# One of VectorE's three operations moved to GpSimd for some score tiles, and the last softmax denominators spread by a shuffle, in an attention block on one core

## The chip, the cores and the metric

The kernel runs on one core of a Trainium2 chip. The metric is the time of one execution on the device in microseconds (us). A profile's span is about 1.8 us shorter than that time. A run over 1.5% above the fastest of its kernel would be called slow. The granted clock of TensorE is the share of its full clock that the trace says it was given.

## The reference

A multi-head attention block, S = 2048 tokens, D = 448, 16 heads of 28:

```python
qkv = (x @ wqkv).reshape(B, S, 3, H, Dh)        # -> q, k, v per head
scores = einsum("bhqd,bhkd->bhqk", q, k) * (Dh ** -0.5)
p = softmax(scores, axis=-1)
o = einsum("bhqk,bhkd->bhqd", p, v)
return o.reshape(B, S, D) @ wo                  # inputs and output bf16
```

## The kernel before

The work is cut into 16 windows (4 groups of 4 heads, times 4 blocks of 512 queries). A window has 16 x 4 = 64 score tiles of 128 keys by 512 queries, 1024 tiles in all. Each tile needs an exponential. ScalarE does most of them, two tiles per instruction (an "exp" below). The others, the "VectorE tiles", go through a cubic polynomial that makes the bits of a bf16 number directly. A VectorE tile takes three VectorE operations and one GpSimd product:

```python
p1 = DVE  tensor_scalar:         DU = SIG/65536 * lo + SIG*(SS - 0.5)      # lo: low 16 bits of the score in PSUM
p2 = DVE  scalar_tensor_tensor:  DV = (lo + const) * DU
gq = POOL tensor_tensor:         DG = DV * DU
f  = DVE  scalar_tensor_tensor:  PTD = (score + const) + DG                # frees the PSUM bank
```

Three PSUM banks (PD) hold VectorE tiles, two double banks (PA) hold pairs for ScalarE, and one bank (PO) collects P times V of a window; its row 28 of each head's 32 rows holds the softmax denominator. The order of all instructions on each engine is fixed while the program is built, by a list scheduler inside the kernel that assumes durations.

The ending of the last window is written by hand. It gathers partial denominators early, so that after the last exp only a reciprocal of 128x16 numbers is left, spread by fp32 matmuls:

```python
for j in range(NKT - NLAST, NKT):            # the last 3 key blocks
    ...                                      # 16 one-column matmuls add to the denominators, then 4 PV matmuls
nc.vector.reciprocal(out=RT[:], in_=gb[:, 0:TPC * HG])       # 128x16
den_expand(0, nc.vector.tensor_copy); den_expand(1, nc.scalar.copy)
...                                          # fp32 matmuls with an identity spread them over the rows
for hf in range(2):
    nc.vector.tensor_tensor(out=OTL[hf][:], in0=OH[hf][:], in1=spread[hf], op=ALU.mult)
    ...                                      # output matmuls; then 2 additions (VectorE), 2 copies (ScalarE), 4 DMAs
```

The softmax here doesn't subtract the row's maximum and nothing guards it: scores larger than these inputs give would overflow.

Of the kernel before, what the change touches and what calls it, by code (L numbers as in the profile page):

```python
# [75 lines left out]
def kernel(  # L76
# [29 lines left out]
    J0 = 10  # L106
    NTAIL = 12
    JL = 6
    DI = 2
    WPE = 1  # L110
    PVM = 0.0
    ADUR = 0.25
# [7 lines left out]
    QEA = 30  # L120
# [6 lines left out]
    O1 = 30  # L127
    O2 = 10
    OF = 0.4
    RV = 2  # L130
# [4 lines left out]
    SPLIT = {2: 4, 3: 2}  # L135
# [3 lines left out]
    UO = 40  # L139

# [32 lines left out]
    DG = [sb([P, QW], F16, f"DG{i}") for i in range(NB)]  # L173
    PARTL = [sb([P, D], F32, f"PARTL{i}") for i in range(2)]
# [15 lines left out]
    ident32 = sb([P, P], F32, "ident32")  # L190
    sel = sb([P, HG], F32, "sel")
    OH = [sb([P, QW // 2], F32, f"OH{i}") for i in range(2)]
    RT = sb([P, TPC * HG], F32, "RT")
    RX = [sb([P, QW // 2], F32, f"RX{i}") for i in range(2)]
# [31 lines left out]
    nc.gpsimd.memset(sel[:], 0.0)  # L226
    for i in range(HG):
        nc.gpsimd.affine_select(out=sel[:, i:i + 1], in_=sel[:, i:i + 1], compare_op=ALU.not_equal,
                                fill=1.0, base=-(HP * i + Dh), pattern=[[0, 1]], channel_multiplier=1)
    nc.gpsimd.memset(ident32[:], 0.0)  # L230
    nc.gpsimd.affine_select(out=ident32[:], in_=ident32[:], compare_op=ALU.not_equal,
                            fill=1.0, base=0, pattern=[[-1, P]], channel_multiplier=1)
# [345 lines left out]
    gbank = [None]  # L578

    def hold(t):  # L580
        free = [s for s in d_slots if s.free_at <= t + 1e-9]
        if free:
            free[0].free_at = 1e18
            gbank[0] = free[0].idx
        return bool(free)

# [7 lines left out]
    def task_part(c, n):  # L594
        due = (12 + c) * WT - PARTD
        for tq in range(n):
# [35 lines left out]
    NLAST = 3  # L632
    NROW = NW * NKT - NLAST
# [24 lines left out]
    def chain_A(fn, deps, acq=None):  # L658
        prev = None
        for tq in range(TPC):  # L660
            prev = add(Op("PE", ADUR, lambda tq=tq: fn(tq), deps=[prev] if prev else deps, prio=-5000 + tq, kind="A",
                          lat=PLAT if tq == TPC - 1 else 0.0, acq=acq if tq == 0 else None))
        return prev

    def den_gather(dst, src, tqs=range(TPC)):
        for tq in tqs:
            nc.tensor.matmul(out=dst[:, tq * HG:(tq + 1) * HG], lhsT=src(tq), rhs=sel[:], start=(tq == 0), stop=True,
                             skip_group_check=True)

    def den_expand(hf, copy):  # L670
        n = TPC * HG // 2
        copy(out=RX[hf][:].rearrange("p (n e) -> p n e", e=HP),
             in_=RT[:, hf * n:(hf + 1) * n].rearrange("p (n o) -> p n o", o=1).to_broadcast([P, n, HP]))

    def den_spread(dst, tqs=range(TPC)):
        for tq in tqs:
            nc.tensor.matmul(out=dst[:, tq * P:(tq + 1) * P], lhsT=RX[tq // 2][:, (tq % 2) * P:(tq % 2 + 1) * P],
                             rhs=ident32[:], start=True, stop=True)

    def partial_sums(pvop):  # L680
        ev = add(Op("DVE", 0.62, lambda: nc.vector.tensor_copy(out=OSB[(NW - 1) % 2][:], in_=PO[:]), deps=[pvop], prio=-5000))
        chain_A(lambda tq: den_gather(PD[gbank[0]], lambda k: OSB[(NW - 1) % 2][:, k * P:(k + 1) * P], (tq,)), [ev], hold)

    def finish_window(w, t):
# [11 lines left out]

        if w >= NW - WPE:
            ev.after = None
            d1 = chain_A(lambda tq: den_gather(PO, lambda k: OSB[b][:, k * P:(k + 1) * P], (tq,)), [ev])
            d2 = add(Op("DVE", 0.17, lambda: nc.vector.reciprocal(out=RT[:], in_=PO[:, 0:TPC * HG]), deps=[d1], prio=-5000))  # L700
            d2a = [add(Op("DVE", 0.25, lambda hf=hf: den_expand(hf, nc.vector.tensor_copy), deps=[d2], prio=-5000)) for hf in range(2)]
            d2b = chain_A(lambda tq: den_spread(PO, (tq,)), d2a)
            d3 = add(Op("DVE", 0.62, lambda: nc.vector.tensor_tensor(out=OT[g][c][:], in0=OSB[b][:], in1=PO[:], op=ALU.mult),
                        deps=[d2b], prio=-5000))
            d3.after = rel
            norm_busy[b] = d3
            ot_done[(g, c)] = d3
            if g == G - 2 and c in SPLIT:
                task_part(c, SPLIT[c])
            if g == G - 1:  # L710
                task_OP(c)
            return
# [19 lines left out]
    def start_tile(n, sop, slot, t):  # L732
# [5 lines left out]
        lo = PX[slot.idx][:].bitcast(U16).rearrange("p (n two) -> p n two", two=2)[:, :, 0]  # L738
        p1 = add(Op("DVE", P1, lambda: nc.vector.tensor_scalar(  # L739
            out=DU[b][:], in0=lo, scalar1=SIG / 65536, scalar2=SIG * (SS - 0.5), op0=ALU.mult, op1=ALU.add),  # L740
            deps=[sop] + prevl, prio=n - O1))
        p2 = add(Op("DVE", P1, lambda: nc.vector.scalar_tensor_tensor(  # L742
            out=DV[b][:], in0=lo, scalar=65536 * (SS - 0.5 + CE / C3), in1=DU[b][:], op0=ALU.add, op1=ALU.mult),
            deps=[p1], prio=n - O2, lat=0.22))
# [377 lines left out]
```

## Time and profile before

| | before |
|---|---|
| time, first 4 runs | 415.99 us median (415.77 to 416.25) |
| span of the profiled run | 414.2 us |
| busy ScalarE / VectorE / TensorE / GpSimd | 97% / 95% / 89% / 54% |
| exps on ScalarE, VectorE tiles | 424, 176 |
| last exp ends, ending after it | 405.21 us, 9.0 us |

The first lines of the page give busy time, share of the span and instructions per engine (PEld is TensorE's weight loading).

```profile
PE 366.8 (89%) x2679; PEld 124.9 (30%) x2679; DVE 395.1 (95%) x699; ACT 399.9 (97%) x439; POOL 224.9 (54%) x210
...
ACT 82%; PE 9%; issue 6%; DMA 1%; DVE 1%; SPq 0%; DVEq 0%
```

The second line is the chain that ended last, by engine: 82% of the span is ScalarE. The table of stretches says why (columns: stretch, its length, then busy time and number of instructions per engine, granted clock of TensorE, share of DMA time, GB/s).

```profile
core 0: us, PE busy (x) PEld busy (x) DVE busy (x) ACT busy (x) POOL busy (x), PEclk, DMA share, GB/s
20.00:400.00 380.00, 338.64 (x2428) 108.87 (x2424) 373.50 (x644) 380.00 (x416) 218.91 (x191) 1.00 0.13 30
...
409.00:411.00 2.00, 0.98 (x6) 0.29 (x3) 1.27 (x3) 0.97 (x2) 0.00 (x0) 1.00 0.02 7
```

ScalarE is busy 380.00 of 380.00 us. VectorE, at 373.50, is nearly full as well. That looks like two bounds, but only one can be read as such: an exp starts every 0.916 us without a gap, so nothing that VectorE or GpSimd does late makes ScalarE wait here. The granted clock reads 1.00. In the view of waits, GpSimd waits for VectorE:

```profile
POOL DG_181 L745 <- DVE DV_175 L742: 35.6, 22, 9.4
```

(35.6 us in total, 22 times, longest 9.4; five more buffers have 23.6 to 29.1 us each.) Last, the ending in order of time (start, duration, engine, line, operation, output<-inputs, number, and in brackets the idle time before it with what ended it).

```profile
403.92 1.29 ACT L934 ACTIVATE PTA_131<-PA_200 128x1024 bf16<-128x1024 f32 x1
...
406.70 0.39 PE L1073 MATMUL PO<-PTA_131,VA_110 128*32 128x512 bf16 x2
406.80 0.26 DVE L1075 RECIPROCAL RT<-PD_201 128x16 f32<-128x16 f32 x1 [1.04 <-PE PD_201 L1069]
...
409.44 0.54 PE L1062 MATMUL PA_199<-WO,OTL_220 128*128 128x448 bf16 x2
...
411.01 0.38 ACTq L1094 DMA_DIRECT2D out_dram<-OUTF_218  x1
```

The last exp ends at 403.92 + 1.29 = 405.21 us; the last PV matmul at 407.09; the span at 414.2.

### The profile page before, as it was taken

The numbers are of one execution on the slowest core, as the hardware profiler recorded it, in microseconds if no ns is written. First come the engines' busy times: TensorE is split into PE (matmuls) and PEld (weight loads), VectorE is DVE, ScalarE is ACT, GpSimd is POOL, SyncE is SP. The second block draws the span as 40 slices with busy tenths as digits, with TensorE's granted clock in tenths as the row PEclk, the third lists the DMA queues.
The fourth block names the chain that finished last, engine by engine and source line by source line (L and its number), as shares of the span: only waits on it lengthen the run. The fifth ranks groups of instructions, "written<-read, shape, count | busy, mean of one in ns | idle before, by whom it ended". The sixth has DMA issues, their size and how long they took to land.

```text
span 414.2 us, 7679 instructions
## 1 busy us (share of the span) xinstructions
PE 366.8 (89%) x2679; PEld 124.9 (30%) x2679; DVE 395.1 (95%) x699; ACT 399.9 (97%) x439; POOL 224.9 (54%) x210
## 2 busy tenths in 40 slices
PE   8988989898898889898897988889898988889995
PEld 5433222323232233323222222222322222222233
DVE  6899999999999999999999999999999999999974
ACT  4999999999999999999999999999999999999992
POOL 3155556474656547475555646456475656656440
PEclk9999999999999999999999999999999999999999
DMA  8410020202201011111400001010410101001012
GB/s 258 80 16 21 3 50 8 55 21 60 65 2 46 0 33 25 26 32 25 97 6 29 18 18 31 2 40 6 91 34 2 46 2 36 10 27 47 18 55 90
DMA packets 33414, 15.85 MB, mean 38 GB/s; under 512 B 26016, under 2 KB 30304, under 8 KB 33376
## 3 DMA queue, kind: packets, MB, share of 16 engines
q1 hardware_dynamic: 32304, 15.05, 14.5%
q8 instruction: 21, 0.34, 0.4%
q10 hardware_dynamic: 1072, 0.32, 0.3%
q14 instruction: 17, 0.14, 0.1%
HBM read 7.37 MB, written 1.96 MB: 23 GB/s over the span
## 4 chain that ended last, share of the span: by engine, by line
ACT 82%; PE 9%; issue 6%; DMA 1%; DVE 1%; SPq 0%; DVEq 0%
ACT PTA_131 L934 4%; ACT PTA_132 L934 4%; ACT PTA_133 L934 4%; ACT PTA_134 L934 4%; ACT PTA_145 L934 4%; ACT PTA_136 L934 4%; ACT PTA_135 L934 4%; ACT PTA_140 L934 4%; ACT PTA_144 L934 3%; ACT PTA_137 L934 3%; ACT PTA_141 L934 3%; ACT PTA_149 L934 3%; ACT PTA_148 L934 3%; ACT PTA_139 L934 3%; ACT PTA_138 L934 3%
## 5 line engine op out<-in xcount | busy, mean ns | idle before, releaser
L745 POOL TENSOR_TENSOR DG_181<-DV_175,DU_169 128x512 f16<-128x512 f16 x30 | 34.6, 1154 | 35.8 <-DVE DV_175 L742 35.6
L745 POOL TENSOR_TENSOR DG_182<-DV_176,DU_170 128x512 f16<-128x512 f16 x30 | 34.6, 1153 | 29.7 <-DVE DV_176 L742 29.1
L745 POOL TENSOR_TENSOR DG_184<-DV_178,DU_172 128x512 f16<-128x512 f16 x29 | 33.5, 1154 | 29.8 <-DVE DV_178 L742 28.5
L745 POOL TENSOR_TENSOR DG_185<-DV_179,DU_173 128x512 f16<-128x512 f16 x29 | 33.4, 1153 | 25.9 <-DVE DV_179 L742 25.8
L745 POOL TENSOR_TENSOR DG_186<-DV_180,DU_174 128x512 f16<-128x512 f16 x29 | 33.5, 1154 | 24.9 <-DVE DV_180 L742 24.7
L745 POOL TENSOR_TENSOR DG_183<-DV_177,DU_171 128x512 f16<-128x512 f16 x29 | 33.4, 1153 | 23.7 <-DVE DV_177 L742 23.6
L649 PEld LDWEIGHTS <-KB_1_94 64*128 64x128 bf16 x256 | 20.8, 93 | 48.2 <-issue 47.3
L649 PEld LDWEIGHTS <-KB_0_91 64*128 64x128 bf16 x256 | 20.5, 93 | 45.8 <-issue 42.1
L649 PEld LDWEIGHTS <-KB_1_92 64*128 64x128 bf16 x256 | 20.2, 93 | 45.8 <-issue 43.9
L649 PEld LDWEIGHTS <-KB_0_93 64*128 64x128 bf16 x256 | 20.5, 93 | 43.8 <-issue 42.7
L934 ACT ACTIVATE PTA_145<-PA_199 128x1024 bf16<-128x1024 f32 x18 | 22.6, 1254 | 0.0
L934 ACT ACTIVATE PTA_144<-PA_200 128x1024 bf16<-128x1024 f32 x18 | 22.5, 1250 | 0.0
L934 ACT ACTIVATE PTA_140<-PA_200 128x1024 bf16<-128x1024 f32 x18 | 22.5, 1249 | 0.0
L934 ACT ACTIVATE PTA_143<-PA_199 128x1024 bf16<-128x1024 f32 x18 | 22.4, 1247 | 0.0
L934 ACT ACTIVATE PTA_139<-PA_199 128x1024 bf16<-128x1024 f32 x18 | 22.4, 1246 | 0.0
L934 ACT ACTIVATE PTA_142<-PA_200 128x1024 bf16<-128x1024 f32 x18 | 22.4, 1242 | 0.0
L934 ACT ACTIVATE PTA_138<-PA_200 128x1024 bf16<-128x1024 f32 x18 | 22.3, 1241 | 0.0
L934 ACT ACTIVATE PTA_141<-PA_199 128x1024 bf16<-128x1024 f32 x18 | 22.3, 1240 | 0.0
L739 DVE TENSOR_SCALAR DU_171<-PD_203 128x512 f16<-128x512 uint16 x29 | 19.9, 685 | 1.0 <-PE PD_203 L649 0.7
L739 DVE TENSOR_SCALAR DU_172<-PD_201 128x512 f16<-128x512 uint16 x29 | 19.8, 682 | 0.9 <-PE PD_201 L649 0.9
L739 DVE TENSOR_SCALAR DU_169<-PD_201 128x512 f16<-128x512 uint16 x29 | 19.8, 684 | 0.5 <-PE PD_201 L649 0.5
L742 DVE SCALAR_TENSOR_TENSOR DV_178<-PD_201,DU_172 128x512 f16<-128x512 uint16 x29 | 19.9, 686 | 0.3
(618 smaller groups left out, 1515.5 us busy)
## 6 DMA issues: line engine op xcount, KB each, us to landing
RRB_195<-SCR_197 SPq DMA_DIRECT2D x8, 256.0 KB
RRB_196<-SCR_198 SPq DMA_DIRECT2D x7, 256.0 KB
KB_1_94<-KB_0_93 SPq DMA_DIRECT2D x4, 128.0 KB
XS_127<-in_x_dram SPq DMA_DIRECT2D x1, 448.0 KB
XS_128<-in_x_dram SPq DMA_DIRECT2D x1, 448.0 KB
XS_129<-in_x_dram SPq DMA_DIRECT2D x1, 448.0 KB
XS_130<-in_x_dram SPq DMA_DIRECT2D x1, 448.0 KB
out_dram<-XS_127 SPq DMA_DIRECT2D x1, 448.0 KB
```

The costliest lines, as they stand in the source:

```text
L649: nc.tensor.matmul(out=ap, lhsT=KB[g % 2][i // 2][a:a + 64, j * P:(j + 1) * P], rhs=QB[w % NQB][i // 2][a:a + 64, :], start=True, stop=Tru ...
L739: p1 = add(Op("DVE", P1, lambda: nc.vector.tensor_scalar(out=DU[b][:], in0=lo, scalar1=SIG / 65536, scalar2=SIG * (SS - 0.5), op0=ALU.mult ...
L742: p2 = add(Op("DVE", P1, lambda: nc.vector.scalar_tensor_tensor(out=DV[b][:], in0=lo, scalar=65536 * (SS - 0.5 + CE / C3), in1=DU[b][:], o ...
L745: gq = add(Op("POOL", PTT, lambda: nc.gpsimd.tensor_tensor(out=DG[b][:], in0=DV[b][:], in1=DU[b][:], op=ALU.mult), deps=[p2], prio=n, kind ...
L934: nc.scalar.activation(out=PTA[pslot.idx][:, 0:len(ns) * QW], in_=PA[s.idx][:, 0:len(ns) * QW], func=ACT.Exp, bias=ACT_BIAS, scale=ACT_SCALE)
```

## The change

The intent: VectorE is nearly as full as ScalarE while GpSimd idles, so for some VectorE tiles GpSimd makes the whole cubic factor and VectorE drops its second operation. A tile is chosen for this when little GpSimd work is queued (XTH), and none of the last 60 tiles is (XEND). In the ending the gathering of denominators and the fp32 matmuls go; VectorE spreads the denominator row by a shuffle inside each group of 32 rows and takes the reciprocal of 128x256 numbers, twice. Four numbers of the scheduler change with it (J0, QEA, O1, RV), and the first three groups' share of the last output rows is partly summed in PSUM (late_sums).

```diff
-    J0 = 10
+    J0 = 9
-    QEA = 30
+    QEA = 20
-    O1 = 30
+    O1 = 20
-    RV = 2
+    RV = 4
+    XTH = 1.5
+    XEND = 60
 ...
+        if pool_load(t) < XTH and n < NT - XEND:
+            p1 = DVE  tensor_scalar   DU = lo/65536 + (SS - 0.5)
+            ga = POOL tensor_scalar   DW = C3*DU + CE
+            gs = POOL tensor_tensor   DV = DU * DU
+            gq = POOL tensor_tensor   DV = DV * DW
+        else:
             p1, p2, gq as before (the product now in place, in DV)
 ...
-    for j in range(NKT - NLAST, NKT): ...          # early denominators, reciprocal of 128x16, fp32 matmuls
     for hf in range(2):
+        cols = slice(hf * hw, (hf + 1) * hw)
+        nc.vector.stream_shuffle(out=DEN[hf][:], in_=PO[:, cols], mask=[Dh] * HP)
+        nc.vector.reciprocal(out=DEN[hf][:], in_=DEN[hf][:])
+        nc.vector.tensor_tensor(out=OTL[hf][:], in0=PO[:, cols], in1=DEN[hf][:], op=ALU.mult)
         for tq in (2 * hf, 2 * hf + 1):
+            nc.tensor.matmul(out=fb[tq], lhsT=OTL[hf][...], rhs=WO[:, g, :], start=(tq not in late_acc), stop=True)
```

(The four operations of the new tile are abbreviated; the rest is cut.)

More of the change, by code (lines that the diff above doesn't have):

```diff
@@ L105 @@
     PBACK = 3
-    J0 = 10
+    J0 = 9
     NTAIL = 12
     JL = 6
+    JACC = 8
     DI = 2
-    WPE = 1
     PVM = 0.0
-    ADUR = 0.25
     PLD = 0.2
@@ L134 @@
     MG = 0.1
-    SPLIT = {2: 4, 3: 2}
+    SPLIT = {2: (0, 1, 2, 3), 3: (2,)}
+    ACCQ = (0, 1, 3)
+    ACCP = 2000
     PARTD = 60
@@ L139 @@
     UO = 40
+    XTH = 1.5
+    XEND = 60
+    PTA1 = 0.62
+    PTQ = 1.04
     x2 = x[0]
@@ L172 @@
     DV = [sb([P, QW], F16, f"DV{i}") for i in range(NB)]
-    DG = [sb([P, QW], F16, f"DG{i}") for i in range(NB)]
-    PARTL = [sb([P, D], F32, f"PARTL{i}") for i in range(2)]
+    DG = DV
+    DW = [sb([P, QW], F16, f"DW{i}") for i in range(2)]
+    PARTL = {tq: sb([P, D], F32, f"PARTL{tq}") for tq in SPLIT[NQC - 1]}
     OSB = [sb([P, QW], F32, f"OSB{i}") for i in range(2)]
@@ L189 @@
     zrow = sb([P, QW], BF16, "zrow")
-    ident32 = sb([P, P], F32, "ident32")
-    sel = sb([P, HG], F32, "sel")
-    OH = [sb([P, QW // 2], F32, f"OH{i}") for i in range(2)]
-    RT = sb([P, TPC * HG], F32, "RT")
-    RX = [sb([P, QW // 2], F32, f"RX{i}") for i in range(2)]
+    DEN = [sb([P, QW // 2], F32, f"DEN{i}") for i in range(2)]
     OUTF = [sb([P, D], BF16, f"OUTF{i}") for i in range(TPC)]
@@ L225 @@
                                 base=-(HP * i + Dh), pattern=[[0, 1]], channel_multiplier=1)
-    nc.gpsimd.memset(sel[:], 0.0)
-    for i in range(HG):
-        nc.gpsimd.affine_select(out=sel[:, i:i + 1], in_=sel[:, i:i + 1], compare_op=ALU.not_equal,
-                                fill=1.0, base=-(HP * i + Dh), pattern=[[0, 1]], channel_multiplier=1)
-    nc.gpsimd.memset(ident32[:], 0.0)
-    nc.gpsimd.affine_select(out=ident32[:], in_=ident32[:], compare_op=ALU.not_equal,
-                            fill=1.0, base=0, pattern=[[-1, P]], channel_multiplier=1)
     for g in range(G):
@@ L576 @@
     ot_done = {}
-    gbank = [None]
-    def hold(t):
-        free = [s for s in d_slots if s.free_at <= t + 1e-9]
-        if free:
-            free[0].free_at = 1e18
-            gbank[0] = free[0].idx
-        return bool(free)
     parts = {}
@@ L595, in task_part @@
         due = (12 + c) * WT - PARTD
-        for tq in range(n):
+        for tq in n:
             task = bank_task()
@@ L631 @@
     NW = G * NQC
-    NLAST = 3
-    NROW = NW * NKT - NLAST
+    NROW = NW * NKT
     rows = {}
@@ L655, in s_ready @@
                 and kmrep[(g, j // TPC, i)].done(t))
-    def chain_A(fn, deps, acq=None):
-        prev = None
-        for tq in range(TPC):
-            prev = add(Op("PE", ADUR, lambda tq=tq: fn(tq), deps=[prev] if prev else deps, prio=-5000 + tq, kind="A",
-                          lat=PLAT if tq == TPC - 1 else 0.0, acq=acq if tq == 0 else None))
-        return prev
-    def den_gather(dst, src, tqs=range(TPC)):
-        for tq in tqs:
-            nc.tensor.matmul(out=dst[:, tq * HG:(tq + 1) * HG], lhsT=src(tq), rhs=sel[:], start=(tq == 0), stop=True,
-                             skip_group_check=True)
@@ L670, in den_expand @@
-    def den_expand(hf, copy):
-        n = TPC * HG // 2
-        copy(out=RX[hf][:].rearrange("p (n e) -> p n e", e=HP),
-             in_=RT[:, hf * n:(hf + 1) * n].rearrange("p (n o) -> p n o", o=1).to_broadcast([P, n, HP]))
-    def den_spread(dst, tqs=range(TPC)):
-        for tq in tqs:
-            nc.tensor.matmul(out=dst[:, tq * P:(tq + 1) * P], lhsT=RX[tq // 2][:, (tq % 2) * P:(tq % 2 + 1) * P],
-                             rhs=ident32[:], start=True, stop=True)
-    def partial_sums(pvop):
-        ev = add(Op("DVE", 0.62, lambda: nc.vector.tensor_copy(out=OSB[(NW - 1) % 2][:], in_=PO[:]), deps=[pvop], prio=-5000))
-        chain_A(lambda tq: den_gather(PD[gbank[0]], lambda k: OSB[(NW - 1) % 2][:, k * P:(k + 1) * P], (tq,)), [ev], hold)
+    late_acc = {}
@@ new lines, in late_sums, with take, f @@
+    def late_sums():
+        def take(tq, n):
+            def f(t):
+                if pos[0] < NT - NTAIL or n and any(o.kind == "B" and o.acq is not None for o in static["PE"]):
+                    return False
+                free = [x for x in d_slots if x.free_at <= t + 1e-9]
+                if not free:
+                    return False
+                free[0].free_at = 1e18
+                late_acc[tq] = free[0].idx
+                return True
+            return f
+        prev = None
+        for n, tq in enumerate(ACCQ):
+            for gg in range(G - 1):
+                prev = add(Op("PE", 0.19, lambda tq=tq, gg=gg: nc.tensor.matmul(
+                    out=PD[late_acc[tq]][:, 0:D], lhsT=OT[gg][NQC - 1][:, tq * P:(tq + 1) * P], rhs=WO[:, gg, :],
+                    start=(gg == 0), stop=False), deps=([prev] if prev else []) + [ot_done[(g_, NQC - 1)] for g_ in range(G - 1)],
+                    prio=ACCP + tq + 0.1 * gg, kind="A", lat=0.0, acq=take(tq, n) if gg == 0 else None))
@@ L695, in finish_window @@
         ev.after = rel
-        if w >= NW - WPE:
-            ev.after = None
-            d1 = chain_A(lambda tq: den_gather(PO, lambda k: OSB[b][:, k * P:(k + 1) * P], (tq,)), [ev])
-            d2 = add(Op("DVE", 0.17, lambda: nc.vector.reciprocal(out=RT[:], in_=PO[:, 0:TPC * HG]), deps=[d1], prio=-5000))
-            d2a = [add(Op("DVE", 0.25, lambda hf=hf: den_expand(hf, nc.vector.tensor_copy), deps=[d2], prio=-5000)) for hf in range(2)]
-            d2b = chain_A(lambda tq: den_spread(PO, (tq,)), d2a)
-            d3 = add(Op("DVE", 0.62, lambda: nc.vector.tensor_tensor(out=OT[g][c][:], in0=OSB[b][:], in1=PO[:], op=ALU.mult),
-                        deps=[d2b], prio=-5000))
-            d3.after = rel
-            norm_busy[b] = d3
-            ot_done[(g, c)] = d3
-            if g == G - 2 and c in SPLIT:
-                task_part(c, SPLIT[c])
-            if g == G - 1:
-                task_OP(c)
-            return
         o1 = [add(Op("SP", 0.6, lambda: nc.sync.dma_start(
@@ L738, in start_tile @@
         lo = PX[slot.idx][:].bitcast(U16).rearrange("p (n two) -> p n two", two=2)[:, :, 0]
-        p1 = add(Op("DVE", P1, lambda: nc.vector.tensor_scalar(
-            out=DU[b][:], in0=lo, scalar1=SIG / 65536, scalar2=SIG * (SS - 0.5), op0=ALU.mult, op1=ALU.add),
-            deps=[sop] + prevl, prio=n - O1))
-        p2 = add(Op("DVE", P1, lambda: nc.vector.scalar_tensor_tensor(
-            out=DV[b][:], in0=lo, scalar=65536 * (SS - 0.5 + CE / C3), in1=DU[b][:], op0=ALU.add, op1=ALU.mult),
-            deps=[p1], prio=n - O2, lat=0.22))
-        gq = add(Op("POOL", PTT, lambda: nc.gpsimd.tensor_tensor(out=DG[b][:], in0=DV[b][:], in1=DU[b][:], op=ALU.mult),
-                    deps=[p2], prio=n, kind="p", lat=PFIN))
+        if pool_load(t) < XTH and n < NT - XEND:
+            p1 = add(Op("DVE", P1, lambda: nc.vector.tensor_scalar(
+                out=DU[b][:], in0=lo, scalar1=1.0 / 65536, scalar2=SS - 0.5, op0=ALU.mult, op1=ALU.add),
+                deps=[sop] + prevl, prio=n - O1, lat=0.22))
+            wb = DW[xn[0] % 2]
+            xn[0] += 1
+            ga = add(Op("POOL", PTA1, lambda: nc.gpsimd.tensor_scalar(
+                out=wb[:], in0=DU[b][:], scalar1=C3, scalar2=CE, op0=ALU.mult, op1=ALU.add), deps=[p1], prio=n - 2, kind="p", lat=0.0))
+            gs = add(Op("POOL", PTQ, lambda: nc.gpsimd.tensor_tensor(out=DV[b][:], in0=DU[b][:], in1=DU[b][:], op=ALU.mult),
+                        deps=[ga], prio=n - 3, kind="p", lat=0.0))
+            gq = add(Op("POOL", PTT, lambda: nc.gpsimd.tensor_tensor(out=DG[b][:], in0=DV[b][:], in1=wb[:], op=ALU.mult),
+                        deps=[gs], prio=n - 4, kind="p", lat=PFIN))
+        else:
+            p1 = add(Op("DVE", P1, lambda: nc.vector.tensor_scalar(
+                out=DU[b][:], in0=lo, scalar1=SIG / 65536, scalar2=SIG * (SS - 0.5), op0=ALU.mult, op1=ALU.add),
+                deps=[sop] + prevl, prio=n - O1))
+            p2 = add(Op("DVE", P1, lambda: nc.vector.scalar_tensor_tensor(
+                out=DV[b][:], in0=lo, scalar=65536 * (SS - 0.5 + CE / C3), in1=DU[b][:], op0=ALU.add, op1=ALU.mult),
+                deps=[p1], prio=n - O2, lat=0.22))
+            gq = add(Op("POOL", PTT, lambda: nc.gpsimd.tensor_tensor(out=DG[b][:], in0=DV[b][:], in1=DU[b][:], op=ALU.mult),
+                        deps=[p2], prio=n, kind="p", lat=PFIN))
         w_, g, c, j, i = tile_of(n)
@@ L769 @@
     d_seq = [0]
+    xn = [0]
     d_last = [None] * NB
@@ L795, in fn @@
                 nc.tensor.matmul(out=PO[HP * st:HP * (st + 1), :], lhsT=VA[g][:, j, st, :], rhs=r["p"][i][1](),
-                                 start=(j == 0), stop=(j == NKT - 1 or w == NW - 1 and j == NKT - NLAST - 1),
+                                 start=(j == 0), stop=(j == NKT - 1),
                                  tile_position=(0, HP * st))
@@ L810, in aft @@
                         st_.free_at = t + SEM
-            if w == NW - 1 and j == NKT - NLAST - 1:
-                partial_sums(op)
-            if j == NKT - 1:
+            if w == NW - 1 and j == JACC:
+                late_sums()
+            if j == NKT - 1 and w < NW - 1:
                 pv_open[0] = False
@@ L1051 @@
     g = G - 1
-    last = acts[-1][2].idx
-    spare = PA[1 - last]
-    gb = PD[gbank[0]]
-    fb = [PD[k][:, 0:D] for k in range(ND) if k != gbank[0]] + [spare[:, 0:D], spare[:, QW:QW + D]]
     hw = QW // 2
-    spread = [PA[last][:, 0:hw], gb[:, hw:QW]]
-    def acc(tq, gs):
-        for gg in gs:
-            lhs = OT[gg][c][:, tq * P:(tq + 1) * P] if gg < g else OTL[tq // 2][:, (tq % 2) * P:(tq % 2 + 1) * P]
-            nc.tensor.matmul(out=fb[tq], lhsT=lhs, rhs=WO[:, gg, :], start=(gg == 0 or tq < 2), stop=(gg == g))
@@ L1064 @@
-    for j in range(NKT - NLAST, NKT):
-        pt = rows[(NW - 1, j)]["p"]
-        for i in range(HG):
-            for tq in range(TPC):
-                col = tq * HG + SI[i]
-                nc.tensor.matmul(out=gb[:, col:col + 1], lhsT=pt[i][1]()[:, tq * P:(tq + 1) * P],
-                                 rhs=VA[g][:, 0, 0, Dh:Dh + 1], start=False, stop=(j == NKT - 1), skip_group_check=True)
-        for i in range(HG):
-            st = SI[i]
-            nc.tensor.matmul(out=PO[HP * st:HP * (st + 1), :], lhsT=VA[g][:, j, st, :], rhs=pt[i][1](),
-                             start=False, stop=(j == NKT - 1), tile_position=(0, HP * st), skip_group_check=True)
@@ L1075 @@
-    nc.vector.reciprocal(out=RT[:], in_=gb[:, 0:TPC * HG])
-    den_expand(0, nc.vector.tensor_copy)
-    den_expand(1, nc.scalar.copy)
-    for hf in range(2):
-        nc.vector.tensor_copy(out=OH[hf][:], in_=PO[:, hf * hw:(hf + 1) * hw])
-    acc(2, range(g))
-    for tq in range(TPC):
-        nc.tensor.matmul(out=spread[tq // 2][:, (tq % 2) * P:(tq % 2 + 1) * P],
-                         lhsT=RX[tq // 2][:, (tq % 2) * P:(tq % 2 + 1) * P], rhs=ident32[:], start=True, stop=True)
-    acc(3, range(g))
@@ L1085 @@
-    for hf in range(2):
-        nc.vector.tensor_tensor(out=OTL[hf][:], in0=OH[hf][:], in1=spread[hf], op=ALU.mult)
-        for tq in (2 * hf, 2 * hf + 1):
-            acc(tq, (g,))
-    for tq in (0, 2, 1, 3):
-        if tq < 2:
+    fb = {tq: PD[late_acc[tq]][:, 0:D] if tq in late_acc else PA[1 - acts[-1][2].idx][:, 0:D] for tq in range(TPC)}
+    for hf in range(2):
+        cols = slice(hf * hw, (hf + 1) * hw)
+        nc.vector.stream_shuffle(out=DEN[hf][:], in_=PO[:, cols], mask=[Dh] * HP)
+        nc.vector.reciprocal(out=DEN[hf][:], in_=DEN[hf][:])
+        nc.vector.tensor_tensor(out=OTL[hf][:], in0=PO[:, cols], in1=DEN[hf][:], op=ALU.mult)
+        for tq in (2 * hf, 2 * hf + 1):
+            nc.tensor.matmul(out=fb[tq], lhsT=OTL[hf][:, (tq % 2) * P:(tq % 2 + 1) * P], rhs=WO[:, g, :], start=(tq not in late_acc), stop=True)
@@ L1091 @@
+    for tq in range(TPC):
+        if tq in SPLIT[c]:
             nc.vector.tensor_tensor(out=OUTF[tq][:], in0=fb[tq], in1=part(c, tq), op=ALU.add)
@@ L1093 @@
             nc.scalar.copy(out=OUTF[tq][:], in_=fb[tq])
-        (nc.scalar if tq == 3 else nc.sync).dma_start(out=out_perm[:, c * TPC + tq, :], in_=OUTF[tq][:])
+        (nc.scalar if tq == TPC - 1 else nc.sync).dma_start(out=out_perm[:, c * TPC + tq, :], in_=OUTF[tq][:])
 _INS = ['x', 'wqkv', 'wo']
```

## The prediction

> **What bounds it now.** ScalarE. In the table of stretches ScalarE is busy 100% from 20 to 405 us; the listing in time order shows exp number 2 starting at 17.27 us and the last of 424 at 403.92 us, so one 128x1024 exp per 0.916 us without a gap. VectorE is close behind (about 98% in the middle), the tensor clock is granted in full, GpSimd is busy 54% and waits mostly for VectorE's second operation (24 to 36 idle us for each of six buffers in the view of waits). The last exp ends near 405.2 us; a tail of 9.0 us follows (span 414.2).
>
> **What the change does, counted in the order of instructions.** VectorE tiles go from 176 to 180, exps from 424 to 422. 57 of the 180 tiles are of the new kind: VectorE drops one scalar_tensor_tensor (0.684 us each, 39 us), GpSimd gains one tensor_scalar and one square. Four added tiles give back about 8 us of VectorE. Net: VectorE busy 395 to about 366 us (88%). GpSimd: a two-input product took 1.154 us here. The Trainium skill ("GPSIMD Engine Reference", Elementwise: side-by-side cycle accounting) gives 2.6 cycles per element for two inputs, 1.11 us at 1.2 GHz for 512 elements, which this trace agrees with, and about 1.03 for short bodies; so I estimate 0.6 to 0.7 us for the tensor_scalar. GpSimd busy then is about 225+57x1.8+4x1.15, or 330 us (80%).
>
> **What reaches the critical path.** Little. VectorE's relief is off the path as long as ScalarE is the bound; how many tiles go to VectorE is held down by three PSUM banks, and a tile of the new kind holds its bank about as long (one VectorE operation less, two GpSimd ones more). Only two exps fewer count: 2x0.916 = -1.8 us. The last exp should end near 403.4 us.
>
> **The tail.** Before, denominators were gathered early, so that only a 128x16 reciprocal remained (0.257 us). Now VectorE does shuffle, reciprocal, product over 128x256, twice, after the last PV matmul, and behind four output additions that PE now feeds only after that matmul. A 16-element reciprocal took 0.245 us against about 0.15 for a one-element operation: some 6 ns per element if it is not pipelined, so 1.6 us for 256 elements (estimate; the skill, "VectorE: DVE Perf Modes", First, the fixed hardware budget, says: an iterative divide with a repeat count of 8). Shuffle and product 0.42 each, as the 128x256 PSUM copies here. Sum from the last exp's end: PV and four additions 3.5, the two chains 5.0, matmul, eviction and DMA 4.3: 12.9 instead of 9.0, +3.9 us. With a pipelined reciprocal (0.4 us) the tail would be about 10.4.
>
> **Prediction.** -1.8 +3.9, or +0.4 if the reciprocal is quick; a little for exps that starve when GpSimd runs late. 417.4 us, 8 in 10 between 413.5 and 421. Faster by over 2%: 0.03; within 2%: 0.93; slower: 0.04.
>
> **What would show it.** Exps still 0.916 us apart and ScalarE at 100% between 20 and 400 us; last exp ending 1.5 to 2 us sooner; VectorE near 88%, GpSimd near 80%; two reciprocals of about 1.6 us; a tail near 13 us.
>
> **What would make it wrong.** GpSimd slower than estimated (tensor_scalar over 1 us): its tiles come late, banks come free late, PE stands before a matmul, and ScalarE starves: several us. Or a pipelined reciprocal and additions that finish before the last exp: then 412 to 414 us.

## The result, and the profile after

| | before | after |
|---|---|---|
| time, 4 runs each | 415.99 us (415.77 to 416.25) | 418.5 us (418.28 to 419.09) |
| ratio of fast runs | | 1.005 (95%: 1.0026 to 1.0074) |
| exps, VectorE tiles (of the new kind) | 424, 176 (0) | 422, 180 (57) |
| last exp ends | 405.21 us | 403.48 us |
| span; ending after the last exp | 414.2; 9.0 us | 416.5; 13.0 us |

Ratios here are the mean time of one kernel's fast runs over that of the other's in the same rounds, so not quite the ratio of the medians quoted. The change made the kernel about half a per cent slower. "The same" by the 2% rule, but clear of noise.

The page of after, first line and chain by engine, and two stretches:

```profile
PE 362.2 (87%) x2609; PEld 121.7 (29%) x2609; DVE 377.6 (91%) x653; ACT 398.2 (96%) x437; POOL 319.9 (77%) x321
...
ACT 83%; PE 7%; issue 5%; DVE 3%; DMA 1%; SPq 0%; DVEq 0%
```

```profile
core 0: us, PE busy (x) PEld busy (x) DVE busy (x) ACT busy (x) POOL busy (x), PEclk, DMA share, GB/s
20.00:400.00 380.00, 335.87 (x2404) 109.54 (x2403) 355.09 (x598) 380.00 (x416) 315.21 (x307) 1.00 0.12 30
...
411.00:413.00 2.00, 0.77 (x2) 0.13 (x2) 1.25 (x3) 0.00 (x0) 0.00 (x0) 0.50 0.34 115
```

Between 20 and 400 us VectorE gave up 18 us of busy time, GpSimd took 96 us more, and ScalarE did exactly what it did before: 416 instructions, 380.00 us busy. That one comparison says that the larger part of the change is off the critical path. The granted clock at the end is new: 0.50. The three GpSimd operations of a new tile, from the view of their lines (durations in ns: least, median, largest):

```profile
L710 POOL TENSOR_SCALAR DW_182<-DU_174 x12: 617/617/618, 66.4 to 369.0; 128x512 f16<-128x512 f16 x12
L712 POOL TENSOR_TENSOR DV_180<-DU_174 x12: 1039/1040/1040, 67.0 to 369.7; 128x512 f16<-128x512 f16 x12
L714 POOL TENSOR_TENSOR DV_180<-DV_180,DW_182 x12: 1151/1154/1157, 68.2 to 370.8; 128x512 f16<-128x512 f16 x12
```

And the ending in order of time, to be set against that of before:

```profile
402.19 1.29 ACT L913 ACTIVATE PTA_143<-PA_195 128x1024 bf16<-128x1024 f32 x1
...
404.01 0.38 PE L774 MATMUL PO<-PTA_143,VA_110 128*32 128x512 bf16 x2
...
404.72 0.62 DVE L605 TENSOR_TENSOR XS_129<-PD_198,KB_0_91 128x448 bf16<-128x448 f32 x1 [5.35 <-PE PD_198 L601]
...
406.33 0.62 DVE L605 TENSOR_TENSOR XS_129<-PD_197,KB_1_92 128x448 bf16<-128x448 f32 x1
...
406.87 0.44 DVE L1035 STREAM_SHUFFLE DEN_203<-PO 128x256 f32<-128x256 f32 x1
...
407.35 1.75 DVE L1036 RECIPROCAL DEN_203<-DEN_203 128x256 f32<-128x256 f32 x1
...
409.13 0.42 DVE L1037 TENSOR_TENSOR OTL_209<-PO,DEN_203 128x256 bf16<-128x256 f32 x1
...
411.75 0.42 DVE L1037 TENSOR_TENSOR OTL_210<-PO,DEN_204 128x256 bf16<-128x256 f32 x1
...
412.58 0.58 PE L1039 MATMUL PD_197<-WO,OTL_210 128*128 128x448 bf16 x1
...
413.76 0.38 ACTq L1045 DMA_DIRECT2D out_dram<-OUTF_208  x1
```

The last exp ends at 403.48. VectorE then runs four additions that belong to the third query block (404.72 to 406.95), because it had stood idle for 5.35 us until TensorE brought their sums; only then comes the shuffle, at 406.87. Two chains of shuffle, reciprocal and product take until 412.17. The last two matmuls take 0.56 and 0.58 instead of about 0.35 us, at half clock.

**Two speeds of the kernel before.** In the three later sessions the kernel before was run 33 times. 18 of these had a mean granted clock of 0.997 or more and took 415.74 to 416.33 us (mean 416.1); 15 had 0.991 to 0.996 and took 417.28 to 418.87 us (mean 417.9). Its first four runs took 415.77 to 416.25. The kernel after, in ten runs, always had 0.992 to 0.996. So the 2.5 us between the medians compare after with the better mode of before; against its other mode after is 0.6 to 1.1 us slower. The ratios in the sessions below use all fast runs of before, both modes.

### The profile page after: what moved, and what is told of

The parts are those of the page before. It is cut to its first block, busy times and chain, and to the rows that moved or that the text cites. A ratio compares the mean times of both kernels' runs of the same rounds, so it can differ in the third digit from the quotient of the medians.

```text
span 416.5 us, 7468 instructions
## 1 busy us (share of the span) xinstructions
PE 362.2 (87%) x2609; PEld 121.7 (29%) x2609; DVE 377.6 (91%) x653; ACT 398.2 (96%) x437; POOL 319.9 (77%) x321
## 4 chain that ended last, share of the span: by engine, by line
ACT 83%; PE 7%; issue 5%; DVE 3%; DMA 1%; SPq 0%; DVEq 0%
ACT PTA_131 L913 5%; ACT PTA_132 L913 5%; ACT PTA_133 L913 5%; ACT PTA_134 L913 4%; ACT PTA_136 L913 4%; ACT PTA_135 L913 4%; ACT PTA_137 L913 4%; ACT PTA_144 L913 4%; ACT PTA_140 L913 3%; ACT PTA_142 L913 3%; ACT PTA_141 L913 3%; ACT PTA_139 L913 3%; ACT PTA_138 L913 3%; ACT PTA_143 L913 3%; ACT PTA_147 L913 3%
## 5 line engine op out<-in xcount | busy, mean ns | idle before, releaser
L634 PEld LDWEIGHTS <-KB_1_94 64*128 64x128 bf16 x256 | 20.5, 92 | 48.9 <-issue 48.0
L634 PEld LDWEIGHTS <-KB_1_92 64*128 64x128 bf16 x256 | 20.5, 93 | 45.5 <-issue 43.6
L634 PEld LDWEIGHTS <-KB_0_93 64*128 64x128 bf16 x256 | 19.6, 92 | 45.2 <-issue 44.5
L634 PEld LDWEIGHTS <-KB_0_91 64*128 64x128 bf16 x256 | 20.0, 93 | 42.8 <-issue 39.6
L723 POOL TENSOR_TENSOR DV_178<-DV_178,DU_172 128x512 f16<-128x512 f16 x23 | 26.5, 1153 | 5.4 <-DVE DV_178 L720 4.4
L723 POOL TENSOR_TENSOR DV_177<-DV_177,DU_171 128x512 f16<-128x512 f16 x20 | 23.1, 1154 | 7.1 <-DVE DV_177 L720 6.9
L723 POOL TENSOR_TENSOR DV_179<-DV_179,DU_173 128x512 f16<-128x512 f16 x20 | 23.1, 1154 | 6.4 <-DVE DV_179 L720 6.4
L723 POOL TENSOR_TENSOR DV_175<-DV_175,DU_169 128x512 f16<-128x512 f16 x21 | 24.2, 1154 | 4.8 <-DVE DV_175 L720 4.1
L723 POOL TENSOR_TENSOR DV_176<-DV_176,DU_170 128x512 f16<-128x512 f16 x21 | 24.2, 1154 | 1.6 <-DVE DV_176 L720 1.1
L723 POOL TENSOR_TENSOR DV_180<-DV_180,DU_174 128x512 f16<-128x512 f16 x18 | 20.8, 1154 | 5.0 <-DVE DV_180 L720 5.0
L913 ACT ACTIVATE PTA_141<-PA_194 128x1024 bf16<-128x1024 f32 x18 | 22.7, 1261 | 0.0
L913 ACT ACTIVATE PTA_140<-PA_195 128x1024 bf16<-128x1024 f32 x18 | 22.7, 1260 | 0.0
L913 ACT ACTIVATE PTA_139<-PA_194 128x1024 bf16<-128x1024 f32 x18 | 22.6, 1258 | 0.0
L913 ACT ACTIVATE PTA_138<-PA_195 128x1024 bf16<-128x1024 f32 x18 | 22.6, 1256 | 0.0
L913 ACT ACTIVATE PTA_142<-PA_195 128x1024 bf16<-128x1024 f32 x17 | 21.5, 1264 | 0.0
L913 ACT ACTIVATE PTA_143<-PA_194 128x1024 bf16<-128x1024 f32 x15 | 18.9, 1263 | 0.0
L913 ACT ACTIVATE PTA_136<-PA_195 128x1024 bf16<-128x1024 f32 x15 | 18.8, 1255 | 0.0
L913 ACT ACTIVATE PTA_137<-PA_194 128x1024 bf16<-128x1024 f32 x15 | 18.7, 1247 | 0.0
L913 ACT ACTIVATE PTA_135<-PA_194 128x1024 bf16<-128x1024 f32 x15 | 18.6, 1241 | 0.0
L913 ACT ACTIVATE PTA_144<-PA_195 128x1024 bf16<-128x1024 f32 x14 | 17.7, 1264 | 0.0
L913 ACT ACTIVATE PTA_148<-PA_195 128x1024 bf16<-128x1024 f32 x14 | 17.6, 1255 | 0.0
L913 ACT ACTIVATE PTA_150<-PA_195 128x1024 bf16<-128x1024 f32 x13 | 16.5, 1271 | 0.0
```

The costliest lines, as they stand in the source:

```text
L634: nc.tensor.matmul(out=ap, lhsT=KB[g % 2][i // 2][a:a + 64, j * P:(j + 1) * P], rhs=QB[w % NQB][i // 2][a:a + 64, :], start=True, stop=Tru ...
L723: gq = add(Op("POOL", PTT, lambda: nc.gpsimd.tensor_tensor(out=DG[b][:], in0=DV[b][:], in1=DU[b][:], op=ALU.mult), deps=[p2], prio=n, kind ...
L913: nc.scalar.activation(out=PTA[pslot.idx][:, 0:len(ns) * QW], in_=PA[s.idx][:, 0:len(ns) * QW], func=ACT.Exp, bias=ACT_BIAS, scale=ACT_SCALE)
```

## The experiments

My theory after reading the two profiles: the main loop became 1.7 us shorter (two exps fewer), and the ending 4 us longer. In that ending the two wide reciprocals take about 2.9 us more than a cheap operation would, and 2.5 us pass between the last PV matmul and the first shuffle. The rivals: the new tiles cost time by themselves, or they are worth far more than two exps and the ending hides it, or TensorE rather than VectorE sets the length of the ending.

Since the ending is the matter, this table gives for each profile when the last exp and the last PV matmul ended, and what followed the last exp to the end of the span:

| kernel | time, median (range) | ratio to before | last exp ends | last PV ends | ending |
|---|---|---|---|---|---|
| before, first profile | 415.99 (415.77 to 416.25) | | 405.21 | 407.09 | 9.0 |
| after, first profile | 418.5 (418.28 to 419.09) | 1.0050 | 403.48 | 404.39 | 13.0 |
| old_tail_new_tiles | 417.83 (415.59 to 418.95) | 1.0015 | 404.15 | 407.59 | 12.1 |
| new_tail_old_tiles | 418.75 (418.67 to 421.68) | 1.0056 | 405.32 | 405.94 | 11.7 |
| reciprocal_taken_out | 416.24 (415.95 to 416.74) | 0.9981 | 404.52 | 405.43 | 9.9 |
| additions_early | 418.55 (417.92 to 419.09) | 1.0036 | 403.93 | 407.03 | 12.8 |
| compact_reciprocal | 416.71 (416.17 to 417.03) | 0.9995 | 404.47 | 405.37 | 10.7 |
| ending_kept_warm | 419.11 (418.43 to 419.13) | 1.0051 | 404.53 | 405.43 | 12.8 |
| additions_early_rest_late | 416.63 (416.34 to 417.37) | 0.9999 | 403.71 | 404.89 | 10.9 |
| all_three | 414.67 (414.28 to 414.85) | 0.9947 | 404.22 | 405.40 | 8.6 |
| after_again | 419.02 (418.78 to 419.31) | 1.0052 | 403.98 | 404.89 | 13.0 |
| after_q30 | 417.73 (417.54 to 418.17) | 1.0021 | 403.91 | 404.51 | 11.9 |
| all_three_q30 | 413.91 (413.78 to 415.88) | 0.9935 | 404.28 | 404.71 | 7.8 |
| all_three_old_tiles | 415.14 (414.83 to 415.41) | 0.9957 | 405.04 | 405.95 | 8.4 |

(Six runs of each, in three sessions of four kernels; 11 runs of before in each session. The sessions ran on three different chips, but the full-clock runs of before had a mean of 416.1 us in each of them, so times of different sessions may be compared to some tenths of a us. Each ratio has a 95% interval of about 0.0025 either way: those of old_tail_new_tiles, reciprocal_taken_out, compact_reciprocal, additions_early_rest_late and, just, after_q30 include 1.)

### 1. The new main loop with the old ending: old_tail_new_tiles

```diff
 (the kernel before)
-    J0 = 10, QEA = 30, O1 = 30, RV = 2
+    J0 = 9, QEA = 20, O1 = 20, RV = 4, XTH = 1.5, XEND = 60
+        if pool_load(t) < XTH and n < NT - XEND: ...      # the new tile, as in the change
```

> The kernel before, with the tiles of the new kind and the four schedule numbers J0, QEA, O1, RV of the change, but its own ending. Its program has 422 exps instead of 424. My theory (main loop worth 2 exps, loss all in the ending): last exp ends about 1.8 us sooner than before (near 403.4 us), ending of about 9.0 us as before, so about 1.8 us faster than before: 414.1 us, ratio 0.9957. Rival 1 (the new tiles themselves cost time, by GpSimd running late): no faster than before or slower, exps further apart than 0.916 us or gaps on ScalarE. Rival 2 (VectorE's relief is worth much more, hidden in the full change by the ending): 5 us faster or more.

The expected 1.8 us did not appear. Among its six runs, the one with full clock took 415.59 us, 0.5 us below the mean of before's full-clock runs (416.1); the others, with clocks of 0.991 to 0.996, took 417.57 to 418.95, like before's slower mode. Its profile shows three things. First, TensorE waited for a DMA at 113 us, and ScalarE lost 0.9 us there (more under 9). Second, the last exp came 1.06 us sooner than before, but the last PV matmul 0.5 us later: TensorE had more left to do. Third, the clock fell while TensorE was recorded as busy all the time:

```profile
core 0: us, PE busy (x) PEld busy (x) DVE busy (x) ACT busy (x) POOL busy (x), PEclk, DMA share, GB/s
407.00:409.00 2.00, 2.00 (x21) 1.44 (x18) 1.21 (x4) 0.40 (x1) 0.00 (x0) 0.70 0.12 42
409.00:411.00 2.00, 2.00 (x10) 1.47 (x9) 0.84 (x2) 0.00 (x0) 0.00 (x0) 0.50 0.00 0
```

In the profile of before TensorE was also recorded as busy for 2.00 of 2.00 us from 407 to 409 us, with the same kinds of matmuls, at a clock of 1.00. From the last PV matmul to the end of the span this profile has 8.6 us, that of before 7.1. That the slower mode of before comes from its ending too fits this, but it is not shown: no slower run of before was profiled.

So the new tiles are not a hidden gain of 5 us, and as far as its one full-clock run shows they are not harmful either. What they are worth could not be read from a kernel whose ending has two speeds.

### 2. The new ending with the old tiles: new_tail_old_tiles

```diff
-    XTH = 1.5
+    XTH = -1.0          # in the kernel after: no tile of the new kind, 424 exps
```

> The kernel after with no tile of the new kind (the threshold set so that none is chosen): 424 exps, 177 VectorE tiles, the new ending. My theory: last exp ends where it did before (near 405.2 us, give or take 0.3), ending of 13.0 us as after: about 4.0 us slower than before, 419.9 us, ratio 1.0096. If the loss of the change lay in the tiles of the new kind, this one would be as fast as before (415.9).

Slower than before without any new tile: the loss lies in the ending. But the size was off: 418.75 instead of 419.9 us. Its exps ended at 405.32, 1.84 us later than in after, yet its shuffle started at 407.35, only 0.48 us later than in after: here one of the four additions ran before the last exp ended. In after, then, most of the 1.8 us that the main loop gained became a longer wait for those additions.

### 3. The cost of the wide reciprocals: reciprocal_taken_out

```diff
-        nc.vector.reciprocal(out=DEN[hf][:], in_=DEN[hf][:])
+        nc.vector.tensor_scalar(out=DEN[hf][:], in0=DEN[hf][:], scalar1=0.0, scalar2=None, op0=ALU.mult)
```

> The kernel after with each of the two 128x256 reciprocals of the ending replaced by a multiplication by 0 of the same tile in place (wrong result in the last 512 rows, on purpose). Theory: each reciprocal of 1.75 us stands on the chain, a multiplication in its place takes about 0.3 us: 2.9 us faster than after, 415.6 us, ratio to before 0.999. Rival (the ending waits for PE's output matmuls and the reciprocals hide behind them): under 1 us faster than after.

The result is wrong on purpose (relative error 0.26).

```profile
408.38 0.29 DVE L1036 TENSOR_SCALAR DEN<-DEN 128x256 f32<-128x256 f32 x1
```

The multiplication took 0.29 us; the ending shrank from 13.0 to 9.9 us. The time fell by 2.3 us from after's first runs and by 2.8 us from its later ones. The reciprocals stand on the chain with their full length. The clock stayed at 1.00 while TensorE worked.

### 4. Output matmuls before the last PV matmuls: additions_early

```diff
-    ... o.kind == "B" and d_inflight[0] >= DI and ...
+    ... o.kind == "B" and (d_inflight[0] >= DI or pos[0] >= NT - NTAIL) and ...
```

> The kernel after, where PE's output matmuls of the third query block, and the first three groups of the last block's, are ordered before the last PV matmuls instead of behind them (one condition of the scheduler). Theory: the four additions on VectorE end before the last PV matmul, so the first shuffle starts when that ends, near 404.5 us instead of 406.87: 2.4 us faster than after, 416.1 us, ratio to before 1.0005. Rival (PE held up by them delays the last exps or the last PV matmuls by as much): no faster than after.

A miss: 418.55 us, nothing gained. In order of time:

```profile
401.37 2.30 DVE L605 TENSOR_TENSOR XS<-PD,KB 128x448 bf16<-128x448 f32 x4 [1.55 <-PE PD L601]
...
403.53 1.88 PE L660 MATMUL PD<-WO,OT 128*128 128x448 bf16 x9
...
407.09 0.44 DVE L1035 STREAM_SHUFFLE DEN<-PO 128x256 f32<-128x256 f32 x1
```

The additions did end at 403.67, as intended. But the scheduler, once those were placed, also put nine other output matmuls (403.53 to 405.41) ahead of the last PV matmuls, which then ended at 407.03 instead of 404.39. The rival was right: in the last microseconds TensorE has no slack either, and what is put ahead of PV must be paid for.

### 5. The same reciprocal, made compact: compact_reciprocal

```diff
-        nc.vector.stream_shuffle(out=DEN[hf][:], in_=PO[:, cols], mask=[Dh] * HP)
-        nc.vector.reciprocal(out=DEN[hf][:], in_=DEN[hf][:])
+        nc.vector.transpose(out=DEN[hf][:], in_=PO[:, cols])                       # 32x32 blocks
+        nc.vector.reciprocal(out=RSM[hf][:], in_=DEN[hf][:].rearrange("p (n e) -> p n e", e=HP)[:, :, Dh])
+        nc.vector.transpose(out=DEN[hf][:], in_=RSM[hf][:]...to_broadcast([P, hw // HP, HP]))
```

After the first transpose the 256 denominators of a head lie as 8 columns on 32 partitions, so the reciprocal has 8 numbers per partition instead of 256. The second transpose reads each of the 8 columns 32 times and so spreads them again.

> The kernel after with the ending's shuffle and 128x256 reciprocal replaced, per half, by a 32x32-block transpose of the PV bank on VectorE, a reciprocal of the 8 columns that then hold the denominators, and a transpose of those 8 columns read with a repeat (right result). Theory: transpose 0.44 as the shuffle, reciprocal of 8 about 0.2, second transpose 0.35 to 0.44: 1.1 us in place of 2.2 per half, so about 2.2 us faster than after, 416.3 us; if TensorE's clock then stays at full, as it did where the reciprocals were taken out, 0.4 us more. Rival (the reciprocals are only a part of a chain that TensorE sets): under 1 us.

Right result, 416.71 us: 1.8 us below after's first runs and 2.3 below its later ones; the ending 10.7 instead of 13.0 us. That is what was expected, and the time is that of experiment 3 within 0.5 us, so nearly all of the reciprocals' cost can be had back.

### 6. Keeping TensorE's clock up: ending_kept_warm

```diff
+        for _ in range((8, 9)[hf]):
+            nc.tensor.matmul(out=PA[last][:, QW:2 * QW], lhsT=zeros[:], rhs=zrow[:], start=True, stop=True)
```

> The kernel after with 8 and 9 matmuls of zeros (128x512, to an unused PSUM bank) on TensorE while VectorE works on the two halves. Theory: the granted clock, which read 0.50 from 411 us on in after, reads 1.00 to the end; the last two matmuls take 0.36 instead of 0.56 to 0.58 us and the last starts 0.19 instead of 0.35 us behind; about 0.4 us faster than after, 418.1 us. Rival 1 (the lower clock cost after more, up to 1.7 us as in the slower runs of before): 416.8. Rival 2 (zeros do not count as activity): clock still 0.50, no change.

```profile
core 0: us, PE busy (x) PEld busy (x) DVE busy (x) ACT busy (x) POOL busy (x), PEclk, DMA share, GB/s
411.00:413.00 2.00, 2.00 (x11) 0.78 (x8) 1.96 (x2) 0.97 (x2) 0.00 (x0) 1.00 0.18 63
```

Matmuls of zeros do count: the clock read 1.00 here, and the means of all six runs were 0.998 to 1.0. The last two matmuls took 0.36 and 0.35 us. The ending became 0.25 us shorter; the time did not become shorter at all (419.11 against 419.02 for after_again), probably since the wait at 113 us (0.72 us here, 0.45 in the profile of after_again) differs as much as that. So in after the lower clock costs little, about 0.25 us where 0.4 was expected: it falls when only two matmuls are left. Both rivals fall.

### 7. Additions early, the rest late: additions_early_rest_late

```diff
 (experiment 4, and)
-                if pos[0] < NT - NTAIL or n and ...
+                if pos[0] < NT - NTAIL or pv_next[0] < NROW or n and ...      # the nine matmuls wait for the last PV
```

> As additions_early, but TensorE's nine matmuls of the last block's first three groups (1.7 us before the last PV matmuls there) come behind the last PV matmul, where VectorE's chain hides them; the four output matmuls of the third block stay early. Theory: the last PV matmul ends near 405.1 us, the four additions are done, and the first shuffle starts then instead of at 406.87: about 1.7 us faster than after, 416.8 us. Rival (anything put ahead of the last PV matmuls costs as much as it saves): as additions_early, 418.5.

```profile
404.95 0.44 DVE L1035 STREAM_SHUFFLE DEN<-PO 128x256 f32<-128x256 f32 x1
```

The first shuffle started 1.92 us sooner than in after. 416.63 us, 1.9 us below after's first runs: a hit, and the rival falls. The order of TensorE's last matmuls is worth as much as the two exps.

### 8. Together: all_three

The edits of 5 and 7, and zeros (2 and 4 matmuls) as in 6.

> compact_reciprocal, additions_early_rest_late and zeros on TensorE (2 and 4) together. If they add up: -2.2 -1.7 -0.4 from after: 414.2 us, about 2 us below the full-clock runs of before (416.1). If not, the ending has a floor of another kind that the profile will show.

414.67 us, with a spread of 0.6 us and clocks of 0.999 to 1.0. The parts nearly add up (414.2 expected). This beats both kernels, 1.4 us below before's full-clock mean and 3.2 us below that of its other mode.

### 9. After, again, and the wait at 113 us: after_again and after_q30

Of the nine profiles with after's main loop (the new tiles and QEA = 20), seven show one gap on ScalarE, at 113 us; the first profile of after and that of additions_early_rest_late do not. after_again is the kernel after unchanged; after_q30 differs in one number:

```diff
-    QEA = 20
+    QEA = 30            # as before the change
```

> The kernel after, unchanged, on the same chip as the other three. 418.3 to 419.1 us as in its first four runs. In the profiles of three kernels with its main loop, TensorE waited 0.4 to 0.9 us at 113 us for a DMA that fills the key tile of the second head group (KB from NK), in that of after it did not: if that wait varies from run to run, the runs here spread by up to 1 us, and last exps end between 403.5 and 404.5 us.

> The kernel after with the number QEA back at 30, as before the change: its program ends the second group's key projections before tile 214 instead of 229 (of 256), 423 exps, 179 tiles. Theory (QEA alone made the keys late): no DMA wait at 113 us; last exp ends near 404.4 us (one exp more than after) without spread; about as fast as after or up to 0.5 us slower than its best runs. Rival (the new tiles make them late): the wait is still there.

after_again took 419.02 us and shows the gap; the line is from its listing of TensorE:

```profile
112.80 0.39 PE L634 MATMUL PA<-QB,KB 64*128 64x512 bf16 x1 [0.46 <-DMA KB<-NK]
```

The first score tile of the second head group waits for the DMA that fills a part of its keys. QEA lets the query projections start earlier; in the order of instructions, with 20 instead of 30 the last key projection of that group stands before tile 229 instead of 214 of 256. In after's trace the operation that feeds this DMA ran at 105.30 us, in before's at 99.78, so 5.5 us of slack were gone. ScalarE then waits between 0.00 and 0.90 us in the nine profiles; that the DMA's own variation decides how long was not measured. In after_q30 the operation ran at 99.94 us again, and the gap is gone. In new_tail_old_tiles, with QEA = 20 and only old tiles, it did not occur either, though that operation ran late there too (104.37 us). So QEA took away the slack; whether the new tiles take the rest is open. The expected time of after_q30 was too high: it took 417.73 us, 1.3 us less than after_again, although it has an exp more. The last exp ends at about the same time in both profiles (403.91 and 403.98 us: the wait that went pays for the exp more). Nearly all of the 1.3 us therefore lies in the ending, 11.9 against 13.0 us: the additions start at 404.02 instead of 405.22 us, in another order of TensorE's last matmuls. The rival (the new tiles make the keys late) falls in its plain form, as the wait went with QEA alone.

### 10. The best, and what the new tiles are worth in it: all_three_q30 and all_three_old_tiles

all_three with QEA = 30, and the same without new tiles (XTH = -1.0):

> all_three with QEA at 30: 423 exps. No wait at 113 us, clock 1.00. Theory: the one exp more (0.92 us) and the wait that goes (0.4 to 0.9 us) nearly cancel: 414.7 us, plus or minus 0.5, as all_three (414.67). Rival: the wait was hidden elsewhere and this is 0.9 us slower, 415.6.

> all_three_q30 without tiles of the new kind: 424 exps, 177 VectorE tiles. What the new tiles are worth when the ending does not cover it. Theory: one exp, 0.9 us slower than all_three_q30, 415.6 us. Rival 1 (VectorE's relief is worth more, additions and evictions come sooner): 2 us slower or more. Rival 2 (nothing, TensorE's PV matmuls of the last window set the end): within 0.3 us of all_three_q30.

all_three_q30 took 413.91 us (one of six runs 415.88, at a clock of 0.990; the others 413.78 to 414.08). It is the fastest kernel, 0.9935 of before. The expectation, 414.7 us give or take 0.5, was missed all the same: the last exp ends as in all_three (404.28 and 404.22 us), but the last PV matmul follows it after 0.43 instead of 1.18 us. QEA had changed the order of TensorE's last matmuls again; this gain was not planned. Its ending:

```profile
404.75 0.45 DVE L1036 STREAM_TRANSPOSE DEN<-PO 128x256 f32<-128x256 f32 x1 [1.72 <-PE PO L775]
405.23 0.20 DVE L1037 RECIPROCAL RSM<-DEN 128x8 f32<-128x8 f32 x1
405.47 0.45 DVE L1038 STREAM_TRANSPOSE DEN<-RSM 128x256 f32<-128x256 f32 x1
405.95 0.42 DVE L1039 TENSOR_TENSOR OTL<-PO,DEN 128x256 bf16<-128x256 f32 x1
...
408.22 0.35 PE L1043 MATMUL PD<-WO,OTL 128*128 128x448 bf16 x1
```

VectorE waits for TensorE's last PV (1.72 us), and starts at 404.75, 0.04 us after it. Without new tiles: 415.14 us, 1.23 us slower. The theory said 0.9 (one exp), the rivals 2 or more, or under 0.3. By time, then, moving VectorE's operation to GpSimd is worth about one exp, 0.3%, in this ending. But only 0.76 us of the 1.23 are an earlier last exp; the rest is the ending (7.8 against 8.4 us), where without the new tiles the last PV matmul came 0.91 instead of 0.43 us after the last exp. In three comparisons now (after_again with after_q30, all_three with all_three_q30, and this one) the ending changed by 0.5 to 1.1 us although no edit touched its code, so this part can't be credited to the new tiles as such.

## Why the prediction was right

The range held the result (418.5 within 413.5 to 421.0; 417.4 was forecast). A range of 7.5 us alone proves little; what speaks for the prediction is that its sum held, term by term. The sum itself is 415.99 - 1.8 + 3.9 = 418.1; the prediction does not say how it came from there to 417.4. (Its "+0.4" for a quick reciprocal is a slip: its own ending of 10.4 us would be +1.4. That branch did not occur.)

- **The bound.** Right. ScalarE was busy 380.00 of 380.00 us before and after, and exps stayed 0.916 us apart.
- **-1.8 us from two exps.** Right in the first profile: the last exp ended 1.73 us sooner, though the first one started 0.17 us later. In the other profile of after the DMA wait took 0.5 us of this. The prediction had the sign of the risk, "exps that starve", but the wrong cause: it named GpSimd being late; it was a number of the scheduler that the prediction did not weigh (whether the new tiles have a part in it is open, see 9). That QEA moved the keys could have been read from the order of instructions beforehand.
- **+3.9 us in the ending.** Right: 13.0 us against 12.9 forecast. Its terms: PV and additions 3.5, measured 3.4 (403.48 to 406.87); the two chains 5.0, measured 5.3; matmul, eviction and DMA 4.3, measured 4.3. Experiments 3 and 5 show the reciprocals on the chain, 7 the additions.
- **The reciprocal.** 1.6 us was worked out from 0.245 us for 16 elements against about 0.15 for one; it took 1.75. The alternative that was left open, a pipelined reciprocal of 0.4 us, is ruled out.
- **GpSimd.** tensor_scalar 0.6 to 0.7 us forecast, 0.617 measured; busy 330 forecast, 319.9 measured, partly because the square took 1.04 and not 1.154 us.
- **VectorE at 88%, 366 us.** Off: 91%, 377.6 us. The step that failed is "VectorE drops one scalar_tensor_tensor (0.684 us each, 39 us)". Back to back, VectorE's operations start 0.60 us apart while each is recorded as 0.68 long. The overlap is counted once, so an operation that is taken out of a full queue saves 0.60 us, and gaps make the others count with their whole 0.68. Summed over all VectorE instructions from 20 to 400 us, the recorded durations fell by 30.5 us (423.7 to 393.2), much as the 39 less 8 of the forecast; but the overlaps among them fell too, from 49.0 to 38.2 us, as the gaps rose from 61 to 127. It touched no time, since VectorE was off the path.
- **What the prediction did not have.** The fall of the clock at the end (about 0.25 us in after), and that before itself has two speeds 1.8 us apart. Compared with all runs of before of a session, the change costs 0.5%; against its full-clock runs, 2.4 to 2.9 us (0.6 to 0.7%).
- **Where a later expectation failed.** From the profiles I read 2.4 us of waiting for the additions and expected all of it back (experiment 4). The wait was real, but the order that removes it takes TensorE time ahead of the last PV matmuls. A wait shows who was late; it does not show that the late one could have come sooner for nothing.

What was only argued: that the three PSUM banks hold down the number of VectorE tiles. No run changed their number. Nor was J0, O1 or RV changed alone, so what these three numbers of the scheduler do is not known.

## What to carry to other kernels

Before unloading an engine that is 95% busy, look whether the one at 100% ever waits for it: here 18 us less of VectorE in the main loop bought one or two exps of 0.92 us. And when an edit changes what a scheduler places, look at the order of the last instructions before crediting the edit: here such reorderings alone moved the ending by 0.5 to 1.1 us. In an ending there is no other work to hide behind, so cost it instruction by instruction, per engine and in order, with the number of elements per partition that a slow operation sees: a reciprocal of 8 columns between two block transposes did in 1.1 us what shuffle and wide reciprocal did in 2.2. And when runs of one kernel fall into two groups, look at the granted clock before explaining a difference of half a per cent.

## What the Trainium skill lacked or had wrong

- "VectorE: DVE Perf Modes" (First, the fixed hardware budget) says that reciprocal is an iterative divide with a repeat count of 8, but no page gives a time, and the perf-mode tier table leaves it out. Here: 0.20 us for 8 elements per partition, 0.245 for 16, 1.75 for 256, all fp32; (1.75 - 0.20) / 248 = 6.25 ns per element, which at the page's 0.96 GHz is 6 cycles (an estimate); the page does not say what its repeat count of 8 means in cycles per element.
- The same page times the shuffle for 2048 elements alone (about 2400 ns), and VectorE's transpose for 128x128 bf16 alone. Here 256 fp32 elements from PSUM took 0.44 us, and a 32x32-block transpose of 256 fp32 elements 0.45 us, from PSUM and also from 8 columns read with a repeat.
- "TensorE: Matmul & The Clock Gate" (Why this matters for your kernels) says to avoid idle gaps of TensorE over about 3 us between matmul bursts. That is not enough: in after the granted clock fell to 0.50 with no gap as long as that, during the second of two gaps of 1.85 and 2.06 us with 0.55 us of matmuls between them; and in old_tail_new_tiles it fell with TensorE recorded busy for 2.00 of 2.00 us, behind one-column matmuls and among small fp32 ones, which in the profile of before ran at 1.00. Its statement in Part 1 that the window runs freely, so that kernels vary by run, fits the two speeds of before (416.1 and 417.9 us on the mean), though no run here shows the window itself. The page doesn't say whether matmuls of zeros count as activity; here they held the clock at 1.00.
- "GPSIMD Engine Reference" (Elementwise: side-by-side cycle accounting) gives 2.6 cycles per element for two inputs, by estimate 1.11 us for 512 at its 1.2 GHz; the product took 1.154 us here, in agreement. It has no figure for two inputs that are the same tile (1.040 us) nor for a tensor_scalar of two operations on 16-bit floats (0.617 us).
